# Another order table for the engines' queues, and a warm-up in small TensorE tiles, in a kernel of two attention and two token-mixing layers

## The chip, the cores and the metric

The kernel runs on one core of one Trainium2 chip. The metric is the time of one execution on the device in microseconds. The engines of the core are TensorE (PE, with its weight loads shown as PEld), VectorE (DVE), ScalarE (ACT), GpSimd (POOL) and SyncE (SP, which issues most of the DMAs here). Each works through a queue of its own, in order, and waits on semaphores for the others.

## The reference

The input x has 2048 rows of 512 values in bfloat16. Four layers are applied in turn, each to a normalised x and added to x: attention, token mixing, attention, token mixing. Both attention layers use the same weights, and so do both mixing layers.

```python
def _A_ref(x, wqkv, wo):
    B, S, D = x.shape
    H = 32; Dh = D // H; W = 256
    qkv = (lambda x, *d: x.transpose(*d))((x @ wqkv).reshape(B, S, 3, H, Dh), 2, 0, 3, 1, 4)
    q, k, v = qkv[0], qkv[1], qkv[2]
    scores = jnp.einsum("bhqd,bhkd->bhqk", q, k) * (Dh ** -0.5)
    idx = jnp.arange(S)
    mask = (idx[:, None] - idx[None, :] >= 0) & (idx[:, None] - idx[None, :] < W)
    scores = jnp.where(mask[None, None], scores, -1e9)
    p = _softmax(scores, axis=-1)
    o = jnp.einsum("bhqk,bhkd->bhqd", p, v)
    return (lambda x, *d: x.transpose(*d))(o, 0, 2, 1, 3).reshape(B, S, D) @ wo

def _B_ref(x, w1, b1, w2, b2):
    h = _layernorm(x, axis=-1)
    u = jnp.einsum("bsd,sf->bdf", h, w1) + b1     # F = 1792
    u = _gelu(u)
    y = jnp.einsum("bdf,fs->bds", u, w2) + b2
    return (lambda x, *d: x.transpose(*d))(y, 0, 2, 1)

x = x + _A_ref(_layernorm(x, axis=-1), A_wqkv, A_wo)
x = x + _B_ref(_layernorm(x, axis=-1), B_w1, B_b1, B_w2, B_b2)
# and both once more
```

## The kernel before, in words

An attention and a mixing layer together are called a layer here; there are two, L = 0 and 1. Attention goes through the 2048 rows in four chunks of 512, Q = 0 to 3, and in each chunk through four groups of heads, t = 0 to 3, and nine steps, m = 0 to 8. That makes 144 steps in a layer. A step is one call of `emit_scores` (PE, L678: two or three runs of key blocks, each as four matmuls in 64x64 tiles, 512 columns in all for Q > 0), one of `emit_exp` (ACT, L689, then the masking of the window's edges on DVE or POOL, L706) and one of `emit_pv` (PE, L727). Scores go to PSUM banks 0 and 1 or 2 and 3 in turn, PV gathers in banks 4 and 5 (`B_O` is 4), and `p_sb` has five slots. Banks 6 and 7 are shared by all other PE steps of the attention; the table `BANKS` says which of the two a step gets.

Beside the steps of a chunk stand the jobs that prepare the next chunk and finish the one before:

- `job_transpose` (PE, L537) turns a normalised tile of 128 rows, and DVE or ACT copies it to `xhT` (L416, L418).
- `job_k` and `job_q` are projections (`project`, PE, L548, four matmuls of 512 columns); `job_v` (PE, L594) is 64 matmuls in 128x32 tiles. The result leaves PSUM through `masked` on DVE (L558) or ACT (L563).
- `job_inverse` and `job_normalise` make the reciprocals of the sums and multiply the output by them (PE L771, DVE L778); `job_outproj` (PE, L642) applies `wo`, adds to x and takes the row statistics (L497); `ln_apply` (L505 to L517) makes the next normalised rows `xh` on DVE, POOL or ACT.

The mixing layer is `job_u` (PE, L850: a column tile ft of 14, in four quarters g of four row tiles each; ACT does gelu, L854) and `job_y` (PE, L865, in two parts; DVE adds to x, L869). In layer 0 half of `job_y` lies beside the attention of layer 1.

At the start SP loads x and `wqkv`, POOL makes constants, and PE runs `WARM` groups of ten matmuls of the identity with itself (`warm`, L491), 128 columns each, into bank 4, while the first rows are loaded and normalised. Nothing reads their result. They stand ahead of the first transposes in PE's queue.

Every piece of work is an operation of the class `Plan`, with the tiles that it reads and writes; from these come the semaphore waits. The order is not found at run time: `ORDER` says in which order the jobs are called, which settles the order of reads and writes on shared buffers and banks, and `LINES` says, for each engine, which operations it has and in which order. An operation that could run on DVE, ACT or POOL runs on the one whose line has it. The weights `w1` and `w2` are loaded into buffers of the attention as they come free; these loads stand in SP's line.

Of the kernel before, what the change touches and what calls it, by code (L numbers as in the profile page):

```python
# [10 lines left out]
P = 128  # L11
# [3 lines left out]
WARM = 13  # L15
# [12 lines left out]
def _table(*text):  # L28
# [5 lines left out]
    'c-pm;Q4YW$2t$3`|Ipk17IlS6hA~kip|sjDp5Qfi`!TJv)32bs^K$bHJ~I$C=A0<wJL4$hn1Ui}Pb=zJ?o;4HBkRRZ-H@oUd3G?yJ!tC6!Ynq&'  # L34
    'l+S7XR1Ag?)l_F8^d&)#;RG12;Cl+PkGj6y*UFKbkodsge@c7tnU7qWmjHG')
ORDER = _table(
    'c-jrrg+dSr6a>KCeYPlApkN@4iY;IwDyWD80v4j!-QC^Y-QC^Y-QC^Yt#|Vg0~myKAd(?DQXmylA`Q~Q5vk#T49Em0q=z%IAtPLn6>i9koNz@J'
    ')I)aUMlN_D2fW}8A9%tW`H=_y$Ok{<MIZ{m7ljdkLMVu$2u2Z9KnWB>5K5sqN@6=gP#U2qgYqbgatK33Bp?Feh(u*nMI}^045}dtZ4irSR7VXo'
    'L@mUl4r-z{;*f}rNJ3rIM<X;qCp1B0^guH-MN9NYbF@Yav_mVjMSF}!XLLYUOhOlQM>q6DFZ9Mx^hF=^!vM^~Kn%iQ48a%-$6O4<D2&8njKFwI'
    '#BPkk6imQmOvhNv!Zggp9L&a4%*O&O#3C%g3@pWR9K|xM!V0X$8f?XStiwjE#U^aP7Hq~g?7#u+!cOeP9$dhF9KuRm#XcOtK^(?$9K#8m#3@|I'  # L40
    '8Jxy7oWogM#3h`^6<o$++{7K+#tq!VE!@QeJj6>p!6Q7yGrYrnJjV+dU*i?t;4Qx46W-%1KH>{L<2!!fCw}7>{(<~}zer9n8B_8P#1u?T2c}_q'
    'W}_q1G6T~w6*JL^8R^W-%*rfup)1{(ojI6`o^+=N3o|FZnVY`!q7VI;hyKjVe2icK3ot(mvJgwKD4Vbd16hp0jAKa#u{cY!6hl~+p)AKTEYC1j'
    'U^pwXDl4%vt1yyLjAsn1F`BWg&Kj)AC2Y;wOkge6VIu3XE|XZF4cL%<*qF`Oh%MNZ&DoNz*oAG`o^9BU9oUhb*_DIYjosOaJ=uf3*^B+ymjl?J'
    'gE){wIfTPFoFh1rlR1eKIf|pXlw&!D<2arZIEB+Wjk7tGvpAP?IG-~)gY&qMi@1P`xq{2MoGZDC8@QHhxSH#@iR-zMo4JMCxShMWle@WtdwGak'
    'd4PL(ga>(yhk2CyxsNA#f~R?l$9alpd4acihL?Dr7kQQEc%7GdjW>9cS9p(id7lsXn2-37Pk4tf_>|B1lF#{uulSB{`JNy6nxFZVpZJkq_?zGO'
    'i{JT^fB2VB8cF|1CD#w8kSUdtDXmf}wH)N8baGT?Wl(xKDU$-^ELUYzR%MZkawwY$Dwnd$L+<iaPI)W0{NyDc`74j|$yY^GKzWs4g;ZE26r|!R'
    's&ECWl!6tak}9KODyJ}os)8!3w5q6*B2-n?R958`ttiE*qGA-O>Z+x9)l?0|s-6;*sM@Nd2CA$2YNUp0qQ**6b2U{nwNzVmS1YwqYqe89wO2>A'
    'P#1MjA9Yh_byW}bR44UPZ}rtg4N!j#)^rWjFb&d34b=z@*C>tA5RKDVjn@Q?)?`i6R87$|t<o&b(Ok{ce9hKk&Co*4(=sj6QmxPet<iF=);g`#'
    '25r<5t=Bef)+TMyc5T&4?a~fi&`#~uZXM7b9o9bW*C8F$5gpeF9o1<a(<z<Q8J*Q_ozr<;(qmoK6<yS2UDI{F(M{dZ9o^ME-PbMs(?dPb6Ft&X'
    'J(Huo)C;}RYkk&pz0+HL(0hH<Cw<X3ebo>B(qDboAN|yC{a=MSTa=l}l3NN(Wyvg!r8EaiZD}pN`C0}`XHJ&MGFoQKV!14<xtfb*GdIg_`7Nip'  # L50
    'TW<5P9Oh-7=40OGXa1Jg@>o6#umV=l3Rz(*VnwZtm9|n=%mOXif~>d&TL~*^Wv!frTbPAfh*h$RR^B44vQ@AuR@JImq{UmT#aMN#VR2T|YFTZo'
    'YYA4z60M%qw<P-y4oQ^b')
LINES = {
    "tensor": _table(
    'c-jTQ2bc)v835q_+uvU^M$QO{y=f5Cj-p2Kpw2wCf|OIMrAFk;OU~xx&MsPt8WGos5JW{NB~~1DE$WDwklOTp%Z2ixLZ}!jh038ys2Zw;>Y+xc'
    '8ES==p+#sOT8B2FUFZ|~g#lq&=o<!y)G#Ncg!GUZW`~ThGAsz|!iumcYziB~_OLeW3>(9?@JaYO><I_M?yx^x3`fJRa55YYC&Jl~6V3#Jt06nw'
    '2$#Z@a6Q}&x59()GTaIG!=oVJ&=B&2L1D-T3Gg};g5ppDMnQQf4dtLJbcb3{52`>-r~{Rt38X+5Xbhd9CnUl&=nF|O4+g>jco$YcGK__xFdW9f'
    'IM@X<;5|r%!!QeGLmDiAg|HbiAp@4fD!2-3VI8c84X_)w!e!V3S+E1{!hZNW)Wdyn6b`}>_y+bsHk^d>kOP<CI9!8VxCyu5dpHA+;2Ctpr@;6U'
    '3>`~iKFo`SurL<HVwixXuqL*^I#?SUVFOIYX7~#XI2oH_du)yEuq$@KMC^_!I0y&g6dZ~}@V7V;GjRfr!ReTWsW=Vi;w+qli!mKH;4;j>Rk#{I'
    '!L_&!|Bah)BW}U%co09wEZmQ~aUUMSukZ*S$76UFFW{$m1<znMUdHQq5-(vc-o{7x0H5Kj#1!ZuKE<2pL}Zko@=#&QM}?>u6{k{En#xfPsz_C-'  # L60
    'JC&i@RFA6AoAeg_jG9stdYf9%eCk9UsS9<b;na&xQ%@R1Ni>w!(+C<u!)P>(qVe<xnnaT+g{IRqnnkIUL9=NNEu?f>PJf}*w2W5KI$BGc>92H|'
    'wo?{uqn)&e_R=o;k`B-zI!1Z;B%PxZbb-!NHeI3|`XA-eExJZG=`P))AL$7_r@+j_&c+3~02krHT#OUA0+;8?+>H}?5Le-<{A=#V{rMdp$=$gZ'
    '*X7<knCtT>9?ea;A-CXR+?t1TGEd+>{5zh=lXw7+;3V$BLwGt*;rBU(XYfp(#dCQc&*ud^h9~nPUd&TDotN+j{2{0DZ2mou<MEuqnY@%Y@-kk>'
    'n|Kwk=0EXP-o|@)FaLuN@j*Vu2lz0b;v;;TPx7~Xp8v}?_$J@y@A)C$<!5Y?%Pg-*UU|wYd8DAA1Suv7Qc7A%QF%?uNM&gyZKamHA(f=M)RPL*'
    'Na{#KX(r93u5^?R(nY#TZ|Nc3B}v-L5a}xeBv}T^1Q{zsWwK0?6qzdHB~9kaESV{DWVI}m6|zW{%V)Ai*2)IiEyrc6te4G_B|GFJ$&jz*gzS{V'
    'a!gLkQ#m8qk}ElKUM|TMDXZVf19>c$<%Zmr7xGXlE9!G`6)m8krbRWs7SiHcMN4RDEv$94f|k<qT0?)TEwqs~)3>z0w$g_BOKqwxwY}EYUuj?M'
    's!2Ln+vqTTM}MOub)0t69@<kU>I6;If%=|K(Gfadr)iqb)7d&*SLza7ri(OPx9Cz`tvmE%{ZzB`kGe*`(A~OM59x8erC;e$J)+-euv2<Y59n1r'
    'tIzbhUeR2=qj&WOeXK9EvXP;=)wBF&R@CxY5i4dTEswonuUk1QZ^f;eRkb&*rq#86*4Ucc&#jTQwr1AR8d##WvJTeGdRto?XuWKJ4YeVbY-6pn'
    '4YT)cyp6MoHq9nkUrV*=_L<GHxt3;&ZH_IqMV4tF*-Bey>ur^7u{E~IHrmIw!_Hfl{ms6xJNBjRwFCA~J7MIf?UY@xi<V>8th#?^H|(C>w)^(L'
    '68)(?u^0Bz3c0%YPds{lFW^PIgeQ1uFY8sjlvngJUcqa6Eg$4{ytX&+M&8_8d42EX&Ag?z@vc6{dwLh|;Yr@d`+0vK@9+8uAL_|I%18S+pX5_~'  # L70
    's?YQp{-J;13w)t3@pRAhrT%AM?;HK1|I0V|X20e?_-()Acl|$p*|YqLpYvV*t)KVL{h;sj!+yzg{klK%hyL6j`D4HD_dMHk{E0tsjSw+j^&9@e'
    'U;2-3(PNAhIp&E)<Et?t7K?dfzE~&bj}>CoSR$5*CF5(cR4f=@iG^a}SU*;a6=U64Hr9-_V&m8(Hji(|2C-G_96Q9;v19BK+s1A&G4_nTV!N0W'
    '`^N#XZ~Q+~R@ia'),
    "vector": _table(
    'c-jrj{c{g=902h5)93wpe`|E}Fk&sw3G)yen-P1kCu|;unp(tM<>Bh$Zd_s~{m@P(?NBLXQ8pYqY-5|XtsxUJc}Nb0@(`V;n0oyIucx6Mw1-d#'
    'hL+F*T0<*n10nDXw1qHe2F;-_ya4@R07OCr421qL2%=#q#6SWJhh#{HkuVm<!DvW>Q7{H3z<8JjGhiuX!X(Ir0$2fYxDHlAJPyarPz<q{fCped'
    'RKQuNg-R%e5qJy|@gyXnU@D%5WDKJ};ScCU9q1Z70L8&L3fp2ZcBU>Aitk`I>`Kp4N1B8KFao>dFwDhnv;;HoHSA8AxE!ZrHm=1SEX8nIiuL#@'
    'F2f=$z)QFe3$YxxV+mfsn>dhu#0uPp4R{1^;cdK*SMUTjVj7*qCQPR>6iQD}FvU?kMbT`ECL|)Jg_J;<^a^EAE-j*L%A%?CF3qJpT0_feGv(6?'
    'DxvfA4Q-<u+C_)xAXU>IDy4IDl#bDLx<NnFBf3LP)P^7bU;afw+?u;`Z|=f<coO&JP8`jHIfj#X1P|kUj^|V!#R;6jvv@MU%2|AzH}PDa$GN<k'
    'SMnPEh(F=)crAa+>-hq2<%_(7FL5RRz*Stw4P3*eT*g6C&dsE`+~q5LkMDDsgh~@X=8kfkA2Nwbh_shp(o_0Le~FMt86;8iq70MaGFajyUSed3'  # L80
    'BuauLNwSQT6iJiOvPFudSk}pUDU=PeNjA%N*&#b+my}3_lu4yjNuAWlVX2n}IU?0^T#m{KX_QlPT7H)^a#haCIk_eG<)&PeJ91f?#5s28o^tJ6'
    'OV`SUxDhVVg}Wq|;<~vgH^fD_SQqCq++;Vw&31F#6t}>=;pVv<_m<0ZGhMzbaOG~FD|S0wh1>1+xYcfr`^;6k{qCVV<{DkCt8r)CNq5<G)(7r}'
    'yYB8e&?i+jNQ1S9_S8^qr319L_R%=)r5&`RM(R`@q*0ozDf+g~(i~0KF*;UX)=ZtO({z!}(G|K_bM*sVs;l%v{ZdzIsqWDY`n7J<Lfxbdx>t{A'
    'k^ZFDbc>>|)?f5{t<gt%TF>fL{YP)>Ieo1E>fh@8Kp*U%_d!0)xA5(JA0O@`{1hMWqkWW5^6CC1pXyWm9G~sq^ke-zKhDqex&A$$<>&kHexWb('
    '<^FxY*XQ|sU*HS<M!(f>^Ba7L-|p-EDPQMr_$puPkNU&@H-EyP_rLl^FBWdM{6xF!TiQKu*4jd?y@gm$>tWq(y7jXNi?K+HwQQSV$(CY?w#+`Z'
    '<(6qfEXRi0d|O~^?JJvUi)^kfwuQFD)?1#fvd`@cE4CurVLNS??Y2@Yv%OYh`>euht<I`!zg1hk9k7FT$PQbtz;l6!K<7Z;z|cT!AS#d;NDGV$'
    'OblcOQUk9CvI74B?$0r!'),
    "scalar": _table(
    'c-jTQ324r77y#h+_`S!U7#bNeCgg}YYN<JvGKDA;b8KN^lI2)AC(YtZvz!xitgNVEt!0#}IT8z-vqpWza+j6Kuy~%qFbGm0879MY$b?z243@)6'
    '*aNu`g9C5^&OjAZLoHl^n{W^AKqEB6D~LlYe1`AP4uBmHVIn4Ae;kBEaTKOv8cxCaxEOOW57**IT91Xe1$SW#OYtzCz_VC|7qABFu?`#XJ~rYr'  # L90
    'Y{58w#BbPvohTGhcS@ur8cP!?ou<)DnoU`>h*nWPZJ_N`LNO|%V^l$vR7KTPOPA>eHP8ckLa*ozy{AvqLG6Sr9B~3Caz9Sy;XH~ba2ikL={%3K'
    'cnPoKd@kTkyp4;vgkyYwkMSw4<SM?zwOr4)_%1)@W`50YIL;sW8@KTv#vmaIJwxx16o!SAFeHo*D?>rZ3E5#y*cT3k&7mk1hw@MwwuXvuEj$We'
    '!;kPQybCU!p_}xQBpE0vGD1>ijHF4rWXN2}l5CkRxsoS^QY6K)Ps*fHj>u^_Cl}<2T$CEAmxt0MFQrA|@?O43yZjT@NPB1>?XSr?Ovh=uPSY7W'
    'M;B<WuGV$BMK|gWjp;!x)pD)S%UY-PdRwpS18vmj`dVA{lYZCV8Z5E|>th3Kuno1*Hr`TgvSnDN&9#NL)bcFf3T?gZwyjoTF)Op9cG8a9Svzml'
    'R%ci3w%xTRdtq<wgMG0!Yq!4!Zr;^<cwbNUAwJwweWFkD44>iiJj)k*j<4{wUf`R2rx*KP-|vUL+)w&>f9lQN<Za&KasT73{@Ee=>0Kg;lA?rY'
    'V3ZjB2koY?kN'),
    "gpsimd": _table(
    'c-jTQdq@^$6bInnIp;m+ynWTOMfXY8Vs>$mw!n&t>W`>ZQ|Pj!ixEcYwye2aSN)@;eL)EoGRkgShKf*YZ59zkh3jHP7nqUJCnVu2D9D%)+w=58'
    'gdq*R;7Fi1`d~7qVg|m$I&8ptl%g0LQG!kQ2H)dblwmQ7uoSydfMxgrNo>Y`>_s)oaTv$(BaUDT>Tnuc(S&U{hwb<iJJ5`ss6+)?(29q+gEpkl'
    'flkb$H<(Xv(T(>Y`ic_7)SL1sjRw*nT1X>l6s1!ZeNNewOF1-|X3!$a<khsC#&Q;y(0JZJrL>tUDM<(EFxAjWYM@4HrmNIK59tZDQ;NE%hm8C2'  # L100
    'Kpw=ycmikhB%a1Ic`h&D<-CjwcqOmqLN4Y_T*BMAij!Q!wS1IMavdMwCO*fP`3B$Pzqy^;_&IlS7x%D9Leiwa43|$NL&iv!d?C3qN9M{r$(Q-E'
# [230 lines left out]
def bass_interleave_layers__sliding_block__mixer_token_mlp__prompt_kernel(  # L332
# [23 lines left out]
    with es:  # L356
# [136 lines left out]
        for n in range(WARM):  # L493
            pe(warm, 1070 if n < 3 else 540, -7.2, reads=[R("ident")], writes=[BK(B_O)])
# [493 lines left out]
```

## Time and profile before

| | |
|---|---|
| median of 3 runs | 529.82 us (528.96 to 530.92) |
| profiled execution | 529.35 us |
| its span, first to last instruction | 527.8 us |
| busy: PE, PEld, DVE, ACT, POOL | 487.1, 279.4, 311.6, 312.0, 190.3 us |
| instructions | 21374 |
| moved by DMA | 40.70 MB, mean 77 GB/s |
| warm-up on PE | 130 matmuls, 1.88 to 10.70 us |

The profiled execution is one run of the program; its time holds the span and 1.55 us around it. PE's busy time is a sum of overlapping matmuls with modelled ends, so 92% of the span does not mean that it works at 92% of its peak. Times inside the trace count from the first instruction.

### The profile page before, as it was taken

How to read it: one execution, taken by the hardware profiler on the slowest of the kernel's cores; microseconds unless marked ns; L12 is line 12 of the kernel's file. 1: busy time of each engine (PE TensorE's matmuls, PEld its weight loads, DVE VectorE, ACT ScalarE, POOL GpSimd, SP SyncE). 2: the span in 40 equal slices, each digit the busy share in tenths (PEclk: the TensorE clock that was granted, in tenths of full speed). 3: DMA queues.
4: the chain of work that ended last, by engine and by line, in shares of the span. 5: the costliest groups of instructions: out<-in, count | busy, mean ns of one | idle time of the engine just before them, and what ended most of it. 6: DMA issues, size and time to landing. Idle time of an engine off the chain costs nothing.

```text
span 527.8 us, 21374 instructions
## 1 busy us (share of the span) xinstructions
PE 487.1 (92%) x9647; PEld 279.4 (53%) x9730; DVE 311.6 (59%) x612; ACT 312.0 (59%) x366; POOL 190.3 (36%) x378
## 2 busy tenths in 40 slices
PE   7898899889887999999899999997998799999997
PEld 7565556656554444445555575555555444444443
DVE  5798788769874440046765786797787634000412
ACT  5787799888999022202578694698799903411000
POOL 5897545654634020001434542383264601000000
PEclk9999999999999999999999999999999999999999
DMA  6182212210023765031003200021222348500761
GB/s 200 44 85 65 66 45 65 66 45 26 26 75 102 180 154 139 1 92 49 4 4 94 73 27 25 2 65 44 66 65 75 106 122 210 140 0 1 208 181 50
DMA packets 68826, 40.70 MB, mean 77 GB/s; under 512 B 5248, under 2 KB 67712, under 8 KB 68736
## 3 DMA queue, kind: packets, MB, share of 16 engines
q1 hardware_dynamic: 64864, 39.33, 26.8%
q0 software_dynamic: 3872, 0.02, 1.3%
q8 instruction: 76, 1.25, 1.0%
q14 instruction: 14, 0.11, 0.1%
HBM read 32.51 MB, written 2.10 MB: 66 GB/s over the span
## 4 chain that ended last, share of the span: by engine, by line
PE 66%; DVE 11%; ACT 10%; issue 7%; POOL 4%; DMA 2%; SPq 0%; ACTq 0%; DVEq 0%; POOLq 0%
PE ps L850 18%; PE ps L865 18%; ACT p_sb L689 9%; PE ps L727 7%; PE ps L678 6%; PE ps L548 5%; PE ps L642 4%; PE ps L594 4%; DVE v_all L558 2%; POOL p_sb L706 2%; PE ps L491 2%; DMA oU<-o 1%; PE ps L537 1%; DVE p_sb L706 1%; DVE o L416 1%
## 5 line engine op out<-in xcount | busy, mean ns | idle before, releaser
L689 ACT ACTIVATE p_sb<-ps 128x1024 bf16<-128x1024 f32 (+8 forms) x288 | 260.1, 976 | 51.4 <-PE ps L678 43.6
L706 POOL TENSOR_TENSOR p_sb<-p_sb,edge 128x256 bf16<-128x256 bf16 (+2 forms) x268 | 125.9, 474 | 159.5 <-ACT p_sb L689 143.3
L678 PE MATMUL ps<-q_sb,k_sb 64*64 64x288 bf16 (+8 forms) x2816 | 108.2, 250 | 7.5 <-ACT p_sb L689 6.3
L727 PE MATMUL ps<-p_sb,v_all 64*64 64x288 bf16 (+8 forms) x2816 | 91.4, 247 | 6.2 <-DVE p_sb L706 1.9
L869 DVE SCALAR_TENSOR_TENSOR x_sb<-ps,b2col,x_sb 128x512 bf16<-128x512 f32 x32 | 24.0, 750 | 122.2 <-PE ps L865 121.3
L678 PEld LDWEIGHTS ps<-q_sb,k_sb 64*64 64x64 bf16 x2816 | 54.2, 106 | 52.5 <-ACT p_sb L689 34.2
L727 PEld LDWEIGHTS ps<-p_sb,v_all 64*64 64x64 bf16 x2816 | 57.2, 107 | 19.8 <-POOL p_sb L706 6.6
L548 PE MATMUL ps<-xhT,wqkv 128*128 128x512 bf16 x217 | 58.1, 380 | 8.1 <-issue 3.8
L865 PE MATMUL ps<-uT,w1buf 128*128 128x512 bf16 x271 | 62.3, 379 | 1.2 <-issue 1.0
L854 ACT ACTIVATE uT<-ps,b1col 128x512 bf16<-128x512 f32 x28 | 18.8, 688 | 49.0 <-PE ps L850 48.9
L507 POOL TENSOR_TENSOR rstd<-vare,mhalf 128x4 f32<-128x4 f32 x16 | 16.2, 1013 | 84.1 <-DVE vare L505 66.4
L706 DVE TENSOR_TENSOR p_sb<-p_sb,edge 128x64 bf16<-128x64 bf16 (+2 forms) x132 | 33.3, 261 | 21.7 <-ACT p_sb L689 15.3
L850 PE MATMUL ps<-xh_sb,w1buf 128*128 128x512 bf16 x186 | 43.5, 379 | 0.9 <-issue 0.5
L865 PEld LDWEIGHTS ps<-uT,w1buf 128*128 128x128 bf16 x280 | 26.7, 98 | 32.7 <-issue 0.7
L497 DVE BATCH_NORM_STATS2 stats<-x_sb 128x6 f32<-128x512 bf16 x64 | 43.3, 685 | 0.9
L558 DVE TENSOR_TENSOR k_sb<-ps,half 128x1024 bf16<-128x1024 f32 x30 | 36.1, 1213 | 5.2 <-PE ps L548 5.2
L558 DVE TENSOR_TENSOR v_all<-ps,even 128x1024 bf16<-128x1024 f32 x28 | 33.9, 1215 | 8.4 <-PE ps L594 8.3
L594 PE MATMUL ps<-wqkv,xhT 128*32 128x128 bf16 x2048 | 35.0, 220 | 4.2 <-issue 3.5
L865 PE MATMUL ps<-uT,oU 128*128 128x512 bf16 x164 | 37.8, 379 | 0.2
L548 PEld LDWEIGHTS ps<-xhT,wqkv 128*128 128x128 bf16 x256 | 20.9, 98 | 28.1 <-issue 4.8
L594 PEld LDWEIGHTS ps<-wqkv,xhT 128*32 128x32 bf16 x2048 | 29.1, 97 | 10.9 <-issue 8.5
L558 DVE TENSOR_TENSOR q_sb<-ps,even 128x1024 bf16<-128x1024 f32 x28 | 34.0, 1214 | 1.2 <-PE ps L548 0.5
(68 smaller groups left out, 431.1 us busy)
## 6 DMA issues: line engine op xcount, KB each, us to landing
w1buf<-in_B_w_dram SPq DMA_DIRECT2D x10, 896.0 KB
oU<-in_B_w_dram SPq DMA_DIRECT2D x6, 896.0 KB
w1buf<-in_B_w_dram SPq DMA_DIRECT2D x10, 512.0 KB, 4.1
oU<-o SPq DMA_DIRECT2D x16, 256.0 KB, 2.6
k_sb<-in_B_w_dram SPq DMA_DIRECT2D x4, 1024.0 KB, 10.1
xhT<-in_B_w_dram SPq DMA_DIRECT2D x2, 1024.0 KB
q_sb<-in_B_w_dram SPq DMA_DIRECT2D x2, 1024.0 KB
out_dram<-x_sb SPq DMA_DIRECT2D x16, 128.0 KB, 4.2
```

Of the source, the lines that this page charges most:

```text
L497: dve(lambda e: e.bn_stats(stats[:, t, :], x_sb[:, t, :]), 690, prio, reads=[R("x", t)], writes=[R("stats", t)])
L548: last = e.matmul(ps[:, b, :], lhsT=wqkv[:, c, c0:c0 + P], rhs=xhT[:, buf, c, :], start=(c == 0), stop=(c == 3))
L558: return e.tensor_tensor(dst, src.unsqueeze(2).to_broadcast([P, n, 2, w]), mask[:].unsqueeze(1).unsqueeze(3).to_broadcast([P, n, 2, w]), o ...
L594: last = e.matmul(acc[32 * a:32 * a + 32, k], lhsT=xhT[:, buf, c, t0:t0 + 32], rhs=wv[:, c, :, a, :], start=(k == 0 and c == 0), stop=(k = ...
L642: last = e.matmul(ps[:, b, :], lhsT=oT[:, buf, t, i * P:(i + 1) * P], rhs=wo_sb[:, t, :], start=(t == 0), stop=(t == 3))
L678: last = e.matmul(ps[64 * c:64 * c + 64, 2 * half + r, 32 * i0:32 * i1], lhsT=k_sb[rows, ring, t, kb % 16, :], rhs=q_sb[rows, t, c, 32 * i ...
L689: exps[plan.job] = plan.op({ACT: (170 + int(2 * (512 - c0) * 0.84), lambda e: e.activation(p_sb[:, slot, :, c0:512], ps[:, 2 * half:2 * ha ...
L706: return e.tensor_tensor(v, v, g, op=ALU.mult)
L727: last = e.matmul(ps[64 * r:64 * r + 64, B_O + (c ^ r), 32 * i0:32 * i1], lhsT=v_all[rows, col:col + 64], rhs=p_sb[rows, slot, r, 32 * i0: ...
L850: r = e.matmul(ps[:, b, :], lhsT=blk[:, sc, (ft % 2) * P:(ft % 2 + 1) * P], rhs=xh_sb[:, sc, :], start=(sc == 0), stop=(sc == NT - 1))
L865: r = e.matmul(ps[:, b, :], lhsT=blk[:, fc, (st % 2) * P:(st % 2 + 1) * P], rhs=uT[:, fc, :], start=(fc == 0), stop=(fc == NFT - 1))
L869: dve(lambda e: e.scalar_tensor_tensor(x_sb[:, st, :], ps[:, b, :], b2col[:, st:st + 1], x_sb[:, st, :], op0=ALU.add, op1=ALU.add), 750, prio,
```

## The change

The tables `ORDER`, `LINES` and `BANKS` are replaced by others. The operations are the same ones, but for the warm-up, and where one could run on several engines the new lines may have it on another: DVE 612 operations before and 605 after, ACT 352 and 353, POOL 374 and 380, SP 126 and 126, PE 941 and 938.

`WARM` goes from 13 groups to 10. Groups 5 to 8 are no longer plain: `first` and `second` use 64x64 tiles (`quads`) and 32x64 tiles (`flats`), `third` mixes 32x64 and 32x32 tiles (`both`), and `fourth` uses sixteen 32x32 tiles (`cells`). They read the identity and write banks 0 to 5; nothing reads their result. In the new line of PE the groups 0 to 8 stand first, then three transposes, then group 9, then the fourth transpose, the first V projection, a Q projection and two K projections, and then the first scores; before it was four transposes, a K and a Q projection, two V projections, scores.

In `job_u` every quarter of the column tiles that use the shared banks (ft % 8 of 6 and 7) is made to read all 16 tiles of `xh`, where it read its own four; in the other column tiles a quarter g reads the tiles of the quarters up to its own.

```diff
-WARM = 13
+WARM = 10
...
-BANKS = _table(
+BANKS = _table(
...
+        wide = ident[:].unsqueeze(1).to_broadcast([P, 4, P])
+
+        def cell(e, row, h, col, w, bank, n=4):
+            return e.matmul(ps[col:col + w, bank, 0:n * P], lhsT=ident[row:row + h, 0:w], rhs=wide[row:row + h, 0:n], start=True, stop=True,
+                            skip_group_check=True, tile_position=(row, col))
+
+        def quads(e, bank):
+            for r in range(2):
+                for c in range(2):
+                    last = cell(e, 64 * r, 64, 64 * c, 64, bank + r)
+            return last
+
+        def flats(e, bank):
+            for a in range(4):
+                last = cell(e, 32 * a, 32, 64 * (a % 2), 64, bank + a // 2)
+            return last
+
+        def both(e, n=4):
+            for a in range(4):
+                cell(e, 32 * a, 32, 64 * (a % 2), 64, a // 2, n)
+                for r in range(2):
+                    last = cell(e, 32 * a, 32, 64 * (1 - a % 2) + 32 * r, 32, 2 + a, n)
+            return last
+
+        def cells(e, n=4):
+            for a in range(4):
+                for c in range(4):
+                    last = cell(e, 32 * a, 32, 32 * c, 32, 2 + a, n)
+            return last
+
+        def first(e):
+            quads(e, 2)
+            quads(e, 4)
+            flats(e, 0)
+            return flats(e, 0)
+
+        def second(e):
+            quads(e, 2)
+            flats(e, 0)
+            quads(e, 4)
+            return flats(e, 0)
+
+        def third(e):
+            both(e)
+            both(e)
+            both(e, 2)
+            return both(e, 1)
+
+        def fourth(e):
+            cells(e)
+            cells(e)
+            cells(e, 2)
+            return cells(e, 1)
         for n in range(WARM):
-            pe(warm, 1070 if n < 3 else 540, -7.2, reads=[R("ident")], writes=[BK(B_O)])
+            tiled = {5: first, 6: second, 7: third, 8: fourth}.get(n)
+            if tiled:
+                pe(tiled, 900, -7.2, reads=[R("ident")], writes=[BK(b) for b in range(6)], mode="cells")
+            else:
+                pe(warm, 1070 if n < 3 else 540, -7.2, reads=[R("ident")], writes=[BK(B_O)])
...
-                pe(f, 870, prio, reads=held + [R("xh", sc) for sc in range(4 * g, 4 * g + 4)], writes=[BK(b)])
+                pe(f, 870, prio, reads=held + [R("xh", sc) for sc in range(NT if ft % 8 >= 6 else 4 * g + 4)], writes=[BK(b)])
```

## The prediction

> **What bounds the kernel now.** I read the page first (shares of busy time, the slices, the chain), then the chain in order of time, then sums per stage, and at the end the weight loads around a change of tile shape.
>
> The page's chain says whose time the span is:
>
> ```profile
> PE 66%; DVE 11%; ACT 10%; issue 7%; POOL 4%; DMA 2%; SPq 0%; ACTq 0%; DVEq 0%; POOLq 0%
> ```
>
> TensorE carries two thirds of it, and no line of a DMA carries more than 1%. The sums per stage (PE, PEld, DVE, ACT, POOL busy; then granted clock, DMA share, GB/s) show where TensorE is not the limit. The stretches are: chunks 1 and 2 of layer 0, its chunk 3, its dense MLP part, chunk 3 of layer 1, and its MLP.
>
> ```profile
> 50.00:94.00 44.00, 40.53 (x1235) 26.44 (x1245) 35.73 (x65) 38.72 (x45) 22.91 (x44) 1.00 0.18 53
> 94.00:134.00 40.00, 36.05 (x1145) 23.90 (x1147) 31.76 (x54) 34.86 (x39) 21.49 (x40) 1.00 0.15 45
> 134.00:168.00 34.00, 28.20 (x838) 17.36 (x844) 25.10 (x54) 32.66 (x36) 17.50 (x31) 1.00 0.27 79
> 168.00:252.00 84.00, 83.09 (x615) 39.23 (x612) 29.03 (x57) 17.02 (x25) 6.46 (x10) 1.00 0.38 97
> 389.00:422.00 33.00, 27.70 (x842) 16.88 (x840) 25.03 (x53) 32.69 (x36) 19.11 (x32) 1.00 0.34 97
> 422.00:528.00 106.00, 101.69 (x541) 46.10 (x544) 23.40 (x40) 13.88 (x19) 2.83 (x5) 1.00 0.42 113
> ```
>
> In chunk 3 of each layer ScalarE is busy for 32.7 of 33 to 34 us: its exponentials set the pace. In the MLP stretches TensorE is busy throughout. Elsewhere both are at about nine tenths. So a delay ahead of all this work moves everything behind it, and there is little slack in which to win it back.
>
> The chain of the first 21 us starts with the warm-up:
>
> ```profile
> 1.88 8.82 PE ps L491 x130
> 10.70 0.24 PE ps L537 x4
> ...
> 13.31 0.82 PE ps L548 x3
> 14.13 0.02 issue
> 14.15 1.24 DVE k_sb L558
> ```
>
> The transposes (L537) stand behind the 130 warm-up matmuls on TensorE. Their rows of xh are ready at 9.0 to 9.5 us (the timeline has DVE's two at 8.29 for 0.73, ACT's at 8.36 for 0.81, POOL's at 8.44 for 1.06). So the end of the warm-up releases the program; whatever lengthens it is paid in full. Its pace, asked of L491 alone:
>
> ```profile
> 1.87:4.87 3.00, 2.99 (x29) 3.00 (x30) 1.00 0.81 265
> 4.87:6.06 1.19, 1.19 (x24) 1.19 (x23) 1.00 1.14 237
> 6.06:10.50 4.44, 4.44 (x84) 4.44 (x81) 1.00 0.95 325
> ```
>
> 29 matmuls take 3.00 us (103 ns each), then the pace is 53 ns for 128 columns, though the clock column says 1.00 all along.
>
> Last, the price of a change of tile shape, in the chain in order of time:
>
> ```profile
> 63.11 0.34 PE ps L678 x12
> 63.46 0.46 PE ps L727 x24
> 63.91 0.22 PE ps L678 x8
> ...
> 276.25 0.97 PE ps L548 x4
> ...
> 279.39 0.33 PE ps L537 x4
> 279.72 0.86 PE ps L548 x4
> ```
>
> A score step (512 columns in 64x64 tiles, four at once) takes 0.22 behind another 64x64 step and 0.34 behind a 128x128 step. A projection takes 0.86 behind a 128x128 transpose and 0.97 behind a 64x64 step. So a change costs 0.11 to 0.12 us each way, and 512 columns stream in 0.86/4 = 0.215 us.
>
> **The warm-up, part by part.** Groups 0 to 4 stay: 50 matmuls, 29 in 3.00 us and 21 at 56 ns, to 6.07. Four tiled groups replace plain ones; groups 10 to 12 go, and group 9 moves in between the transposes.
> - `first`: two quads and two flats, each 512 columns with four tiles at once: 4 x 0.215, and two changes of shape (128 to 64x64, 64x64 to 32x64) at 0.12: 1.1 us, to 7.2.
> - `second`: the same four, shapes alternating, four changes: 1.3, to 8.5.
> - `third`: for each of four rows one 32x64 tile and then two 32x32 tiles, that is eight stretches of alternating shape in a call of `both`, and four calls with 4, 4, 2 and 1 times 128 columns. The trace has no mixture of small shapes. Dear end: each alternation costs as the changes above. Streaming is 8 x 0.215 x (4+4+2+1)/4 = 4.7 us and 32 changes x 0.115 = 3.7: 8.4 us. Cheap end: all 12 tiles, which cover disjoint cells, run at once. Then 0.59 us of streaming, but 48 pairs of load and matmul; L594 issues 65 pairs in 0.93 us (sum over 16.60 to 17.53), so 0.7 us. I take the dear end: both changes of shape that the trace shows cost 0.11 to 0.12, and none is free.
> - `fourth`: 64 matmuls, sixteen 32x32 tiles at once: 0.59 of streaming, 0.9 by the pace of L594.
>
> The end of the tiled groups is 6.07 + 1.1 + 1.3 + 8.4 + 0.9 = 17.8 us by the dear end, 10.1 by the cheap one, against 10.70 for the warm-up now. The rule of the Trainium skill, page "TensorEngine Tiling (Array Packing)", section "Key Properties", is that a change of the tiling mode, not of the tile alone, drains the engine (its list of configurations has 32x64 and 32x32 apart). By that rule `third` is serial; the trace agrees for the two pairs of shapes that it has (0.11 and 0.12 us), and shows nothing of the third.
>
> From there to the first exponential I go through the new order with durations of these rows: transpose 0.31; copy 0.46; the third transpose, which waits for the first one's bank, 0.46; the plain group 0.56; the last transpose 0.22; V projection 1.01; ACT's mask of it 1.30, which frees the bank for the K projection, 1.10; DVE's mask 1.26; scores 0.49. That is 7.2 us after the tiled groups. The timeline has the first exponential at 18.94. It would start at 17.3 by the cheap end and at 25.0 by the dear one. Carried on to the seventh exponential of the first tile (its end stands at 26.6 now), the new order, with V masks spread over the exponentials, gives 25.7 and 33.4: 0.9 less or 6.8 more.
>
> Can the loss be won back? DVE's and ACT's next work stands in their queues behind the copies of the transposes, so they wait too; only POOL's constants (`spread`, `put_ones`) run ahead: 0.3 us.
>
> **The order table.** Counted in the programs, TensorE's work is the same: 288 score and 288 PV steps, 64 projections, 259 changes of shape before and 258 after. What moves:
> - In each layer two more projections stand behind the first score of chunk 3 (6 to 8, 3 to 5). There TensorE has room. Each is 0.95 us; best case -3.8, worst 0 since chunks 0 to 2 are nearly as full of ACT work: -1.0 taken.
> - ACT gets three more normalisations of xh, one fewer copy, two fewer masks; one normalisation (0.7) falls in chunk 3 of layer 0: +0.7.
> - DVE is busy 28.2 of 30 us from 20 to 50; the new order has ten masks fewer on it (132 to 122) and some 2.6 us less work on it by the end of chunk 0: -1.0 (0 to -2).
> - Behind the last `normalise`, one u step (0.86) instead of two stands ahead of `outproj`. DVE needs 1.3 us for the two multiplications between them, so TensorE waits 0.6, once a layer: +0.8 (0 to 1.2).
> - The added reads in `job_u` (ft 6 and 7 wait for all of xh): they stand behind a u step on group 3, which waits for the same rows: nothing.
> Net -0.5, between -5 and +3, as the stages' slack allows.
>
> **Sum.** +6.8 - 0.3 - 0.5 = +6.0. The profiled execution took 529.35 (span 527.8 and 1.55 around it): 535.35; the median is 0.47 above it, so I say 535.5.
>
> **Rivals.**
> 1. The small shapes run at once, as their cells are disjoint. For: four 64x64 tiles of a score step do (512 columns in 0.22). Against: every change of shape in the trace costs 0.11. Then -0.9 - 0.5: 528.5, and with the order's span 524 to 531. It is faster than before, and decides as soon as `third` takes under about 2 us.
> 2. The order table is worth more: chunk 3's gaps (5.8 us of idle TensorE in layer 0, 5.3 in layer 1) are filled by the four moved projections and DVE's relief counts in full: -4.5 beside the dear warm-up (+6.5): 532.
> 3. In `third` two of sixteen cells' width is at work at a time, and the engine falls back to the 103 ns pace of the first 3 us: streaming doubles, +4.7: 540. For: that pace exists while the clock column reads 1.00. Against: no later stretch shows it.
>
> **Chances.** A measurement here can tell about 0.5% (2.6 us). Dear warm-up with a neutral order 0.55 (its own range 531 to 539): slower in 0.47 of it, same 0.07, faster 0.01. Rival 1, 0.28: faster 0.13, same 0.12, slower 0.03. Rival 2, 0.12: same 0.07, slower 0.03, faster 0.02. Rival 3, 0.05: slower. Sums, rounded: faster 0.16, same 0.26, slower 0.58. The range 526 to 539.5 leaves out the better part of rival 1, and rival 3.
>
> **What would show it.** In the new profile: the lines of `cell` end near 17.8 us and the matmuls of `both` stand in alternating stretches 0.33 apart; the first exponential starts near 25; from the seventh on, stages are as long as now, chunk 3 still bound by ACT; TensorE idles 0.6 us ahead of the last `outproj`. It is wrong if the tiled groups end near 10, or if stages later than 30 us differ by more than 3 us in sum.

## The result, and the profile after

The changed kernel takes 539.16 us (median of 4 runs, 538.43 to 539.53) against 530.08 us (528.96 to 530.92) for the kernel before: a ratio of 1.0171, 95% interval 1.0148 to 1.0194. It is slower by 9.1 us. Its profiled execution took 539.5 us, with a span of 538.0 us.

The page of the changed kernel gives TensorE 77% of the chain, where it had 66%. The second line is the granted clock in 40 slices of 13.45 us each, in tenths; before, it was full from its first record to TensorE's last matmul.

```profile
PE 77%; ACT 8%; DVE 5%; POOL 5%; issue 4%; DMA 0%; SPq 0%; POOLq 0%; ACTq 0%; DVEq 0%
...
PEclk9699999999999999999999999999999999999999
```

The 6 in the second slice is the news. The sums for the stages that were shown of before (TensorE, its weight loads, VectorE, ScalarE and GpSimd busy; then clock, DMA share, GB/s) are chunk 3 of layer 0, its mixing part, chunk 3 of layer 1 and its mixing part:

```profile
144.50:179.80 35.30, 31.58 (x876) 18.45 (x876) 24.68 (x48) 34.97 (x38) 23.41 (x45) 1.00 0.26 76
179.80:262.70 82.90, 82.47 (x538) 38.25 (x536) 28.26 (x56) 16.80 (x23) 4.09 (x6) 1.00 0.37 98
397.20:432.60 35.40, 31.25 (x864) 18.17 (x863) 26.12 (x54) 34.77 (x38) 21.17 (x38) 1.00 0.32 91
432.60:538.00 105.40, 101.61 (x541) 45.82 (x540) 23.53 (x41) 12.09 (x17) 2.11 (x3) 1.00 0.43 114
```

Chunk 3 is still bound by ScalarE (35.0 of 35.3 us, 34.8 of 35.4), and the mixing parts by TensorE. So the loss is to be looked for ahead of them: the first exponential starts at 29.91 us, 11.0 later than before. The same sums for TensorE alone, over the plain groups 0 to 4, `first` and `second`, `third` in two pieces, `fourth`, the transposes with the plain group 9, and what follows to the first exponential:

```profile
2.20:7.53 5.33, 5.32 (x50) 1.00 0.88 254
7.53:9.98 2.45, 2.45 (x34) 1.00 1.09 365
9.98:14.36 4.38, 4.38 (x25) 1.00 0.22 73
14.36:19.93 5.57, 5.57 (x27) 0.50 0.00 0
19.93:21.33 1.40, 1.40 (x67) 0.50 0.00 0
21.33:24.60 3.27, 3.09 (x40) 0.50 0.00 0
24.60:29.91 5.31, 4.54 (x93) 1.00 0.01 3
```

Three things are to be seen. `third` lasts from 9.98 to 19.93. From 14.36 to 24.60 the granted clock is 0.50, although TensorE is busy without a gap in the first two of these rows. And all 50 plain matmuls are slow ones, 107 ns each, where the profile before had 29; the column reads 1.00 there, but the trace has no clock record ahead of the first rise, so in that row it says nothing. The weight loads in `third` show its alternation, and where each stretch waits ("issue" names no other engine):

```profile
11.26 0.10 PEld L497 LDWEIGHTS ps<-ident 32*64 32x64 bf16 x1 [0.23 <-issue]
11.59 0.09 PEld L497 LDWEIGHTS ps<-ident 32*32 32x32 bf16 x2 [0.23 <-issue]
11.90 0.10 PEld L497 LDWEIGHTS ps<-ident 32*64 32x64 bf16 x1 [0.23 <-issue]
12.23 0.09 PEld L497 LDWEIGHTS ps<-ident 32*32 32x32 bf16 x2 [0.23 <-issue]
```

A 32x64 tile and a pair of 32x32 tiles start every 0.31 to 0.33 us. The forecast had 0.33.

### The profile page after: what moved, and what is told of

Its sections match the earlier page's. It is cut to its first block, busy times and chain, and to the rows that moved or that the text cites. A ratio compares the mean times of both kernels' runs of the same rounds, so it can differ in the third digit from the quotient of the medians.

```text
span 538.0 us, 21591 instructions
## 1 busy us (share of the span) xinstructions
PE 510.0 (95%) x9804; PEld 283.2 (53%) x9804; DVE 312.8 (58%) x605; ACT 312.3 (58%) x365; POOL 192.1 (36%) x384
## 4 chain that ended last, share of the span: by engine, by line
PE 77%; ACT 8%; DVE 5%; POOL 5%; issue 4%; DMA 0%; SPq 0%; POOLq 0%; ACTq 0%; DVEq 0%
PE ps L923 18%; PE ps L908 18%; PE ps L736 10%; PE ps L785 8%; PE ps L606 8%; ACT p_sb L747 7%; PE ps L700 5%; PE ps L652 4%; PE ps L497 3%; POOL p_sb L764 2%; DVE oT L836 1%; PE ps L595 1%; PE ps L829 1%; PE ps L491 1%; DVE v_all L616 1%
## 5 line engine op out<-in xcount | busy, mean ns | idle before, releaser
L764 POOL TENSOR_TENSOR p_sb<-p_sb,edge 128x128 bf16<-128x128 bf16 (+2 forms) x278 | 130.3, 473 | 149.8 <-ACT p_sb L747 135.9
L785 PE MATMUL ps<-p_sb,v_all 64*64 64x288 bf16 (+8 forms) x2816 | 92.8, 247 | 7.1 <-POOL p_sb L764 3.3
L606 PE MATMUL ps<-xhT,wqkv 128*128 128x512 bf16 x256 | 65.8, 381 | 0.7 <-ACT v_all L621 0.5
L923 PE MATMUL ps<-uT,w1buf 128*128 128x512 bf16 x280 | 64.1, 380 | 0.0
L764 DVE TENSOR_TENSOR p_sb<-p_sb,edge 128x256 bf16<-128x256 bf16 (+2 forms) x122 | 31.5, 267 | 25.4 <-ACT p_sb L747 19.7
L908 PE MATMUL ps<-xh_sb,w1buf 128*128 128x512 bf16 x192 | 44.7, 380 | 0.3 <-ACT p_sb L747 0.3
L616 DVE TENSOR_TENSOR k_sb<-ps,half 128x1024 bf16<-128x1024 f32 x30 | 36.2, 1214 | 5.6 <-PE ps L606 5.3
L616 DVE TENSOR_TENSOR v_all<-ps,even 128x1024 bf16<-128x1024 f32 x29 | 35.3, 1221 | 5.9 <-PE ps L652 5.7
L575 ACT ACTIVATE xh_sb<-x_sb,shift,rstd 128x512 bf16<-128x512 bf16 x12 | 9.5, 810 | 49.2 <-POOL shift L569 49.2
L923 PE MATMUL ps<-uT,oU 128*128 128x512 bf16 x168 | 38.1, 379 | 0.0
L616 DVE TENSOR_TENSOR q_sb<-ps,even 128x1024 bf16<-128x1024 f32 x29 | 35.1, 1214 | 4.1 <-PE ps L606 4.1
```

The lines of the kernel that those rows point to most:

```text
L606: last = e.matmul(ps[:, b, :], lhsT=wqkv[:, c, c0:c0 + P], rhs=xhT[:, buf, c, :], start=(c == 0), stop=(c == 3))
L616: return e.tensor_tensor(dst, src.unsqueeze(2).to_broadcast([P, n, 2, w]), mask[:].unsqueeze(1).unsqueeze(3).to_broadcast([P, n, 2, w]), o ...
L764: return e.tensor_tensor(v, v, g, op=ALU.mult)
L785: last = e.matmul(ps[64 * r:64 * r + 64, B_O + (c ^ r), 32 * i0:32 * i1], lhsT=v_all[rows, col:col + 64], rhs=p_sb[rows, slot, r, 32 * i0: ...
L908: r = e.matmul(ps[:, b, :], lhsT=blk[:, sc, (ft % 2) * P:(ft % 2 + 1) * P], rhs=xh_sb[:, sc, :], start=(sc == 0), stop=(sc == NT - 1))
L923: r = e.matmul(ps[:, b, :], lhsT=blk[:, fc, (st % 2) * P:(st % 2 + 1) * P], rhs=uT[:, fc, :], start=(fc == 0), stop=(fc == NFT - 1))
```

## The experiments

Theory A: the tiled groups hold up the program, because shapes that alternate run one after another and because the granted clock falls while few cells of the array work; the order table is worth little. Its rivals are named with each run. "New" and "old" are the order tables, "plain" and "tiled" the warm-up. Times are medians in us; each ratio is to runs of the kernel before on the same chip beside it, and is what kernels are compared by, since the kernel before itself gave medians of 527.2 to 531.2 from one set of runs to the next. The changed kernel's own ratio is 1.0171.

| run | time | before | ratio, 95% interval |
|---|---|---|---|
| new_plain | 531.14 | 529.54 | 1.0023, 1.0001 to 1.0045 |
| old_short | 526.28 | 529.54 | 0.9935, 0.9915 to 0.9954 |
| old_tiled | 541.92 | 529.54 | 1.0223, 1.0184 to 1.0261 |
| third_sorted | 529.71 | 529.54 | 1.0005, 0.9985 to 1.0025 |
| third_one_place | 542.36 | 528.84 | 1.0261, 1.0236 to 1.0285 |
| third_full | 537.91 | 528.84 | 1.0175, 1.0147 to 1.0203 |
| new_bias_early | 529.47 | 528.84 | 1.0011, 0.9995 to 1.0028 |
| old_bias_early | 526.92 | 528.84 | 0.9966, 0.9953 to 0.9979 |
| new_spread_later | 529.98 | 528.91 | 1.0016, 0.9998 to 1.0033 |
| new_u_reads | 529.92 | 528.91 | 1.0019, 0.9998 to 1.0040 |
| new_two_masks | 528.39 | 527.22 | 1.0029, 1.0010 to 1.0048 |
| new_both_moves | 530.17 | 531.20 | 0.9991, 0.9967 to 1.0014 |

### Order and warm-up apart: new_plain, old_short, old_tiled

```diff
# new_plain, against the changed kernel
-            tiled = {5: first, 6: second, 7: third, 8: fourth}.get(n)
+            tiled = None
# old_short, against the kernel before; old_tiled has this and the tiled groups 5 to 8
-            pe(warm, 1070 if n < 3 else 540, ...)
+            pe((lambda e: warm(e, 1)) if n > 9 else warm, 1070 if n < 3 else 540, ...)
```

> The changed kernel with groups 5 to 8 plain again, so that its warm-up is 90 plain matmuls in the new order. Theory A (the tiled groups hold up the program: changes of shape that cost 0.115 us each, and a granted clock that falls to half because few cells work; the new order itself is worth about -1.7 us): the warm-up ends near 9.8 us if the pace rises after 50 matmuls and near 8.3 if after 29, the rows are there at 9.3, the clock column stays at 1.00, the first exponential starts 13 us sooner than in the changed kernel (29.9), and the total is 526 to 528 us. Theory B (the new order carries the loss, by POOL's constants and V masks in chunk 0, and the tiles mostly lie beside it): the total stays at 536 or more.

> The kernel before with groups 10 to 12 cut to one matmul each: 103 plain matmuls in the old order. Both theories: the warm-up ends near 9.2 to 9.4, where the rows set the start, in place of 10.7: 528.7 us. It is the base for the order table: by theory A the run with the new order and 90 plain matmuls is some 1.7 us faster than this one, by theory B it is 7 or more slower.

> The kernel before, in its old order, with the four tiled groups in place of its plain groups 5 to 8 and one matmul in each of groups 10 to 12. Theory A: the tiled groups take as long as in the changed kernel and end near 21 us, with the clock at half from about 14 us to 24; the total is some 11 us above the kernel before: 541. Theory B: the tiles alone cost little, 532.

The tiles cost 1.5% in the new order (1.0171/1.0023) and 2.9% in the old one (1.0223/0.9935). Theory B, in which the tiles cost little, is gone, and old_tiled is where theory A had it. But theory A missed too: new_plain was to be at 526 to 528 us, and below old_short. It is above it, by 1.0023/0.9935 = 1.0089, some 4.7 us. So beside a plain warm-up the new order costs time. old_short was 2.4 us better than expected, though its warm-up ended at 10.0 and not at 9.4; in its profile chunk 0 is 2.0 us shorter than in the kernel before, with the same order, and why stays open. The stages say where (us, from profiles; exponentials by their ends):

| stage | before | after | old_short | new_plain |
|---|---|---|---|---|
| start to first exponential | 20.0 | 30.9 | 19.5 | 18.5 |
| chunk 0, first to last exponential | 35.5 | 38.1 | 33.5 | 37.9 |
| chunks 1 to 3, from one last exponential to the other | 113.8 | 110.7 | 114.6 | 111.7 |
| to the first exponential of layer 1 | 83.5 | 84.1 | 83.5 | 84.1 |
| chunk 0 of layer 1 | 44.2 | 45.5 | 44.1 | 45.1 |
| chunks 1 to 3 of layer 1 | 125.7 | 123.2 | 123.9 | 123.6 |
| to the last step of `job_y` | 101.7 | 102.2 | 102.2 | 102.9 |

In both pairs (before and after, old_short and new_plain) the new order loses 2.5 to 4.4 us in chunk 0 of layer 0, gains 2.9 to 3.1 in its chunks 1 to 3, and loses 1.0 to 1.3 in chunk 0 of layer 1. The pair with tiled warm-ups, old_tiled and the changed kernel, has 36.2 and 38.1 us for chunk 0, 112.9 and 110.7 for chunks 1 to 3.

This loss and this gain are in part the same work in another place. In the new order 18 projections are copied out of PSUM during chunk 0 and 26 in chunks 1 to 3, in the old one 16 and 28, and in the new order one exponential of chunk 1 stands ahead of the last one of chunk 0. In the plain pair TensorE is busy 2.2 us more in this stretch (34.17 against 31.93) and 3.1 us less in chunks 1 to 3 (102.5 against 105.6). At the last exponential of layer 0 new_plain's profile is only 0.5 us behind old_short's (168.1 against 167.6). The profiles also show less of the loss than the medians do: new_plain's profiled execution took 528.58 us and old_short's 526.02, 2.6 apart, where the ratios give 4.7.

### What `third` costs, and why: third_sorted, third_one_place, third_full

Each replaces the body of `third` in the changed kernel.

```diff
# third_sorted: the same matmuls, by shape
+            for n in (4, 4, 2, 1):
+                for a in range(4):
+                    cell(e, 32 * a, 32, 64 * (a % 2), 64, a // 2, n)
+                for a in range(4):
+                    for r in range(2):
+                        last = cell(e, 32 * a, 32, 64 * (1 - a % 2) + 32 * r, 32, 2 + a, n)
# third_one_place
+            for n in (4, 4, 2, 1):
+                for _ in range(14):
+                    last = cell(e, 0, 32, 0, 64, 0, n)
# third_full: per call, four times the four 64x64 tiles, then the four 32x64 tiles
```

> The changed kernel with the same matmuls in `third`, but sorted by shape: four 32x64 tiles, then eight 32x32 tiles, so two stretches a call in place of eight. Theory A (a change of shape makes stretches serial; tiles of one shape on disjoint cells run at once): `third` takes 2 x 0.215 x 2.75 + 8 x 0.115 = 2.1 us in place of 9.95, half of the cells work, the clock stays at 1.00, and the total is 529 to 530 us. Rival D (any small tiles run one after another, whatever their shape): twelve stretches, 12 x 0.215 x 2.75 = 7.1 us, the clock falls as before, and the total is 536 to 538.

Its sums for TensorE over `first` and `second`, `third`, and `fourth`:

```profile
6.55:8.90 2.35, 2.35 (x34) 1.00 1.06 362
8.90:11.00 2.10, 2.10 (x68) 1.00 0.70 223
11.00:11.85 0.85, 0.85 (x72) 1.00 0.00 0
```

`third` takes 2.0 us (8.94 to 10.93), close to the 2.1 worked out from 0.215 and 0.115 us, and the clock stays up through the warm-up. The same 48 matmuls, sorted, cost a fifth of the 9.95 us. Rival D is gone, and with it rival 1 of the prediction: tiles of one shape do run at once, tiles of two shapes don't.

> The changed kernel with `third` as 14 stretches a call of one 32x64 tile in one place: no change of shape inside, two of sixteen cells at work. Theory A (the granted clock follows how much of the array works over stretches of 3.41 us; it fell where at most 0.33 of the cells' time was used and stayed where at least 0.37 was): here 2/16 = 0.125, so the clock falls to half 3.4 to 6.8 us after `third` begins, `third` takes 10 to 12.5 us instead of 14 x 0.215 x 2.75 = 8.3, the total is 538 to 542. Rival C (what lowers the clock is the emptying at each change of shape): no change, no fall, 8.3 us, total 535 to 537.

> The changed kernel with `third` as eight stretches a call that alternate between four 64x64 tiles (all cells) and four 32x64 tiles (half of the cells): as many changes of shape as in the changed kernel, but 0.75 x 0.215/0.33 = 0.49 of the cells' time used. Theory A: the clock stays at 1.00, `third` takes 4.7 + 32 x 0.115 = 8.4 us instead of 9.95, the transposes run at full pace, and the total is 534 to 536. Rival C (the changes of shape lower the clock): it falls as in the changed kernel, and the total is 538 to 540.

The stretches with `third` in them, first of third_one_place, then of third_full (TensorE busy, clock):

```profile
9.45:13.29 3.84, 3.84 (x22) 1.00 0.44 141
13.29:22.20 8.91, 8.91 (x40) 0.50 0.00 0
```

```profile
9.93:18.60 8.67, 8.67 (x132) 1.00 0.06 21
18.60:19.66 1.06, 1.06 (x72) 1.00 0.06 15
19.66:27.20 7.54, 6.23 (x127) 1.00 0.01 2
```

One tile in one place, with no change of shape and no gap, brings the clock down (at the end of the first stretch of 3.41 us that lies wholly in `third`, which took 12.8 us; that and the total of 542.36 are just above what was expected); 32 changes of shape with more cells at work do not. Rival C is gone; how much of the array works fits all three. third_full shows the change without the fall: `third` 8.7 us, and 7.5 us from the transposes to the first exponential where the changed kernel needed 8.6.

The total of third_full is a miss, though: 537.9 and not 534 to 536. Its profile has three half-clock stretches of 3.41 us later on (from 34.7, 113.2 and 174.7 us), and the one run of it with a mean clock of 0.999 took 536.39. So what the clock's fall costs is read from the profiles, up to the first exponential; in the totals it does not show (ratios 1.0175 and 1.0171).

### What the new order loses in chunk 0: five runs

VectorE works more there. The sums over chunk 0 of new_plain, then of old_short (TensorE, weight loads, VectorE, ScalarE, GpSimd), and who keeps ScalarE waiting in each (total, times, longest):

```profile
sum 38.90, PE 35.20 PEld 22.62 DVE 35.57 ACT 30.81 POOL 30.03; mean PE 11.73 PEld 7.54 DVE 11.86 ACT 10.27 POOL 10.01
...
ACT p_sb L747 <- PE ps L736: 9.4, 11, 2.3
```

```profile
sum 34.50, PE 32.39 PEld 20.13 DVE 31.75 ACT 29.19 POOL 29.34; mean PE 10.80 PEld 6.71 DVE 10.58 ACT 9.73 POOL 9.78
...
ACT p_sb L689 <- PE ps L678: 3.6, 7, 1.1
```

The first candidates were GpSimd's two bias loads (28.2 to 32.0 us with the gap ahead of them) and its row of `spread` constants ahead of a mask.

```diff
# new_bias_early, old_bias_early: the two loads no longer read spread, and
+_bias = _pool[44:46]        # 54:56 in the old order
+del _pool[44:46]
+_pool[9:9] = _bias
# new_spread_later, on top of new_bias_early: eight constants set between later masks
+_spread = [_pool[n] for n in (34, 36, 38, 39, 40, 41, 42, 44)]
```

> The kernel with the new order and a plain warm-up, with POOL's two loads of the bias columns moved from behind its constants in chunk 0 (28.1 to 32.0 us there, ahead of the masks of the second tile) to the front of its queue, where it waits for the first rows. Theory E (in the new order these loads hold masks, so that TensorE's PV and the scores behind it are late and ACT starves 2.3 us): the eighteenth exponential comes some 2 us sooner and the total falls from 531.1 to 528.5 to 529.5. Rival F (other work of the new order holds chunk 0, or the early loads collide with those of x): 531 or more.

> The kernel with the old order and 103 plain matmuls, with the same two loads moved to the front of POOL's queue. Theory E: the loads stand behind more masks there (30.8 to 33.3 us) and hold less: 0.5 to 2 us faster than the 526.3 of the same kernel without the move, so 524.3 to 525.8. Rival F: no faster than 526.

> The kernel with the new order, a plain warm-up and the early bias loads (529.5), with eight of POOL's constants (`spread`) moved behind the masks of its chunk 0 and then set between the masks of the second tile. In the new order five of them stand in a row ahead of a mask for which DVE's queue waits 1.28 us (27.9 to 29.2), and from there DVE has no gap to 40 us. Theory G (this row of constants is what the new order loses in chunk 0): the eighteenth exponential comes 1 to 1.5 us sooner than 38.07 and the total is 528.0 to 528.8. Rival H (DVE's own share of the work sets chunk 0, and the masks only move the gap): within 0.5 us of 529.5.

With the early loads the eighteenth exponential came 0.5 us sooner, not 2, and chunk 0 took 37.2 us instead of 37.9. The totals of new_plain and new_bias_early can't be told apart by their ratios: 529.47 lies in theory E's range, but the kernel before beside it was faster too. In the old order the move gained nothing; it seems to cost 0.3%, though the intervals just touch. In its profile (528.55 us, where the median is 526.92) the first exponential came 1.4 us later (20.9), behind a half-clock stretch from 12.9 to 16.3. Moving the constants brought nothing (chunk 0: 37.7 us). Theories E and G fall. Then VectorE:

```diff
# new_two_masks: two V projections from VectorE's line to ScalarE's
+_act.insert(24, _dve.pop(69))
+_act.insert(20, _dve.pop(64))
# new_both_moves: this and the early bias loads
```

> The kernel with the new order and a plain warm-up (531.1), with two V projections of chunk 0 masked on ACT in place of DVE: those that DVE finished at 29.5 and 33.6 us there. Between the first and the last exponential of chunk 0 DVE is busy 35.6 of 38.9 us in the new order, and 31.8 of 34.5 in the old one (17 projections copied out by DVE, against 15), while ACT waits 9.4 us for scores. Theory I (the new order has put more work on DVE in chunk 0 than the old one, and DVE sets its pace): that stretch falls from 37.9 to 35.5 to 36.7 us, and the total by 1 to 2.4 us to 528.7 to 530. Rival H2 (the order of TensorE's queue sets it, whoever copies): the stretch stays within 0.6 us, and the total at 531.

> The kernel with the new order and a plain warm-up, with both moves: POOL's two bias loads at the front of its queue, and two V projections of chunk 0 masked on ACT. Each alone left chunk 0 as long as it was (37.2 and 37.7 us from its first to its last exponential, 37.9 without): without the loads the chain ran over DVE without a gap from 29.3 to 40 us, without the two masks it ran over the loads from 28.2 to 31.9. Theory J (two holds side by side, of which each covers the other): with both gone the stretch falls to 35 to 36.5 us, close to the old order's 33.5. Rival H2 (the order of TensorE's queue itself sets chunk 0): 37 or more.

Chunk 0 took 37.7 us with two masks moved and 37.2 with both moves: theories I and J fall too. (The median of 528.39 for two masks is not theory I's gain: the kernel before took 527.22 beside it, and the ratio is 1.0029.) VectorE was 2.4 us less busy there (33.1 us), and little came of it. What is left is TensorE's own queue (H2): the work that it has more in this stretch, 2.2 of the 4.4 us, and its order, which none of these runs changed. That the order makes up the rest is argued by exclusion, not shown.

### The added reads: new_u_reads

```diff
-... for sc in range(NT if ft % 8 >= 6 else 4 * g + 4)]
+... for sc in range(4 * g, 4 * g + 4)]
```

> The kernel with the new order and a plain warm-up (531.1), with the added reads of `job_u` taken out again: each quarter reads its own four tiles of xh. The prediction said that the added reads cost nothing: within 0.5 us of 531.1, and the time between the last exponential of the second layer and its last u step stays 63.2 us. Rival: TensorE waits there for rows that it does not use, and both fall by 0.3 us or more.

The ratios (1.0019, 1.0023) can't be told apart. In the profile, 65.1 us lie between the two points named, but a half-clock stretch (420.7 to 424.1) falls into them; from the last PV step to the last u step it is 61.6 us in both. The reads cost nothing.

The fastest version is old_short, with the old order and a shorter plain warm-up: 526.28 us, 0.65% below the kernel before.

## Why the prediction was right, step by step

**Direction and mechanism** held: slower, through a warm-up whose end releases the program, and past it through `third`, whose alternating shapes run one after another. The forecast was 535.5, the result 539.16. That this lies inside the range, 0.3 us from its end, is in part luck: up to the seventh exponential the forecast was 5.0 us short, and what followed gave 0.9 of that back. The last step of the sum was also off: 535.35 and 0.47 are 535.8, not 535.5. The steps on the way (us):

| step | predicted | measured |
|---|---|---|
| plain groups end | 6.07 | 7.6 |
| `first` and `second` | 2.4 | 2.4 |
| `third` | 8.4 | 9.95 |
| `fourth` | 0.9 | 1.4 |
| from there to the first exponential's start | 7.2 | 8.6 |
| first exponential starts | 25.0 | 29.9 |
| seventh exponential's end, against before | +6.8 | +11.8 |
| everything after it | about -0.8 | -1.7 |

**The term that was mis-sized** is the tiled part at a constant pace. The change of shape was priced well: third_full, which makes 32 of them at full clock, took 8.7 us for the 8.4 worked out, and third_sorted 2.0 for 2.1. But rival 3 came true in part. It had named the right cause, few cells at work at a time, gave it 0.05 and put it at 540. The pace did halve, though not from the start of `third` but at 14.36 us, and it stayed so past the tiles: `fourth`, the transposes and the plain group 9 ran at half clock as well. Against the predicted steps that is 1.55 + 0.5 + 1.4 = 3.45 us. Against third_full, whose clock stayed up in these steps, it is 1.3 + 0.3 + 1.0 = 2.6 us; the other 0.8 or so was priced too low at full clock. "No later stretch shows it" was read from a trace in which no stretch used so little of the array.

**The plain groups** were 1.5 us late. TensorE started at 2.21 in place of 1.88, since GpSimd's new queue makes `ident` later, and the rise of the pace came 5.3 us after the start, where the profile before had 3.0. I took one profile's 29 slow matmuls as a property of the kernel. In the 14 profiles it comes 3.0 to 6.0 us after the first matmul, in kernels that begin alike, so the profile before was at the lucky end.

**The order table** was to be worth -0.5; from the first exponential to the last step of `job_y` the two profiles give 504.5 and 503.7 us, -0.8. That agreement is luck in its parts. The relief of VectorE between 20 and 50 us (-1.0) didn't come: by the end of chunk 0 it has done 3.0 us more work than before (46.1 against 43.1), where 2.6 less was counted, and in chunk 0 the new order has it busier (35.6 of 38.9 us against 31.8 of 34.5 in the plain pair). The gain in the later chunks was larger than the -1.0 taken (2.9 to 3.1 in layer 0). And beside a plain warm-up the same order costs 0.9%, near 4.7 us, past the +3 of the bounds. Beside the tiles the same order gains 0.5% (1.0171/1.0223), some 2.7 us. Why the two differ isn't settled: in the profiles 1.8 us of the difference lie ahead of the first exponential (30.9 against 33.6 in the tiled pair, 18.5 against 19.5 in the plain one), and single profiles of one order differ by up to 3 us behind it.

**TensorE's wait ahead of `outproj`** is there. The chain of the changed kernel in layer 1 runs from the second `job_inverse` over VectorE's two multiplications:

```profile
441.84 0.60 PE ps L829 x32
442.44 0.02 issue
442.46 1.30 DVE oT L836 x2
443.76 0.04 issue
443.81 1.90 PE ps L700 x8
```

Of the 1.36 us between the two TensorE rows one u step covers 0.86; TensorE waits 0.4 to 0.5, not 0.6.

**The added reads** cost nothing, as said. **Win-back** by work that ran ahead was put at 0.3: old_tiled, in the old order, is 13.65 us later than the kernel before at its first exponential and 13.4 at the last step.

## What to carry to other kernels

A warm-up is only worth what it does for the clock, and it stands ahead of everything: end it when the first operands are there, and keep enough of the array at work in it (here the clock fell where about 0.36 of it or less was used). Count tile shapes like instructions: sort small tiles by shape, so that a change of shape (0.11 to 0.12 us here) is paid once per group and not per tile. An order table's worth is not read from busy sums: taking 2.4 us from the busiest engine of chunk 0 left the chunk as long as it was. And before two orders are compared by the length of a stage, count the work that each puts into it.

## What the runs showed of the hardware

In these profiles the granted clock follows the share of the array that works, over stretches of 3.41 us. Every half-clock stretch inside a program is 3.41 us or a multiple of it (10.24 in the changed kernel). I summed, for each such stretch, the matmuls' streaming time (53 ns for 128 columns, twice that at half clock) times their tile's share of 128x128, and divided by 3.41 us. Of the fourteen falls in the fourteen profiles, up to TensorE's last matmul, thirteen came after a stretch with at most 0.345, one after 0.375; no stretch that kept the full clock was below 0.358. This counts from the recorded starts; by the modelled ends the clock fell after up to 0.391 and stayed after as little as 0.344, so the border is near 0.36 and not known more closely than some 0.03. The time with any matmul streaming does not separate them: the clock fell after 0.99 of it (third_one_place, 0.124 of the array) and stayed after 0.39. Nor is it a matter of the warm-up alone. In third_sorted it fell in chunk 0, behind a stretch in which TensorE was busy 1.5 of 3.4 us:

```profile
32.62:36.04 3.42, 1.54 (x80) 1.00 1.32 125
36.04:39.45 3.41, 3.41 (x44) 0.50 1.36 6
```

In some kernels such falls go with longer runs. Of new_plain's twelve runs the five with a mean clock of 0.999 or more took 529.09 us at the median, and the five at 0.994, which is two such stretches, 531.56. Of old_short's twelve the four with one fall took 525.69, the eight without 526.57, so falls are not all that makes runs differ.

The Trainium skill, page "TensorE: Matmul & The Clock Gate", section "What's actually happening", has the monitor look at a free-running window of 3413 ns, and the clock drop after an idle window. The trace agrees on the window: half-clock stretches last 3.413 us or a multiple of it. It differs on "idle" if that means that no matmul runs: in third_one_place TensorE never paused, and the clock fell. The measurement decides.

A change between 32x64 and 32x32 tiles costs as much as one between 64x64 and 128x128 did before: 0.31 to 0.33 us a stretch, of which 0.215 is streaming.
